# Attention with a gated feed-forward on one core: norm steps through PSUM, kept transposes, stored weight sums and another order of loads in the front stage

## The chip, the cores and the metric

One core of a Trainium2 chip runs the whole program in one launch. The metric is the device time of one execution in microseconds (us). Before the change three timed executions took 1230.99, 1231.0 and 1231.91 us, a median of 1231.0.

## The reference

The input `x` has 2048 rows of 512 in float32. With `xn` its layer norm (epsilon 1e-5, no scale or offset), the output is `x + s * g`:

```python
qkv = xn @ wqkv                      # 512 x 1536, 32 heads of 16
p = softmax(q @ k.T * 16 ** -0.5)    # every head, 2048 x 2048, no mask
s = (p @ v) @ wo                     # 512 x 512
h = relu(xn @ w1 + b1) ** 2          # 512 x 1792
g = silu(h @ w2 + b2)                # 1792 x 512
```

All inputs and the output are float32.

## The kernel before

Every large matrix product is made in three terms: an operand is cast to a "high" part in fp32r, what is left is its "low" part, and high x high, high x low and low x high are added up in PSUM. A split is thus a cast (mostly on ACT) and a subtraction (mostly on POOL).

The program has a **front stage** that normalizes x, transposes it and makes k, q and v, and then 64 **turns** of attention, into which the feed-forward network's matmuls are woven, and a short end. The order of every engine is written out by hand: an engine runs its instructions in the order in which the Python code issues them and waits by semaphore for what each needs. SP issues nearly all DMAs, also in order, and a DMA that waits holds those behind it.

The front stage works on four chunks of 512 rows:

- `norm` (L176) takes statistics on DVE (L181, L187), a square root on ACT (L191), then for each group of rows a few steps on numbers of 128x2 (L193 to L198: a reciprocal, one Newton step, the offset), all on DVE with operands in SBUF (`rs`, `mv`). From chunk 1 on ACT applies them as scale and offset (L204, tile `T`). It is a generator: the caller sets with `next` where the pieces stand among other work.
- `transpose` (L227) turns 256 rows by eight TensorE transposes into two PSUM tiles `D`, casts the high part on ACT (L238) and subtracts on DVE (L243). `transpose_tile` does so for the first two blocks of chunk 0, through a PSUM tile `B`. Even chunks lie in `KA0` (high) and `KA1` (low), odd ones in `xh`, `xl`.
- v is made per 128 rows by twelve matmuls (`start_value`, `end_value`, L117), evicted to one of three blocks `P10` to `P12` and stored (`vd`).
- k and q of a pair of chunks (0 and 1, then 2 and 3) are made by a scheme of seven products in place of eight (the Winograd form of Strassen's). It needs four sums of weight quarters for each of four kinds, k and q by two halves p (`sums_w`, L340 to L343, DVE; split by `split_sums`, L110), and four sums of transposed x (`sums_x`, L311 and L326 on DVE, cast L320, low part POOL L311). `first_products` and `second_products` work on the even chunk alone (L377, L388), `last_products` makes the rest for one kind: five groups of six matmuls (L291) with six DVE additions (L415) that free the PSUM banks, each result split (L104, L110) and stored (`kd`, `qd`).

PSUM tiles `B` and `D` have four banks each, taken in turn. `first_half(c)` holds what is done for the odd chunk c: products of the even chunk, splits of sums, transposes, x sums and values. After `first_half(1)` come the four `last` of the first pair, with chunk 2's norms, transposes and values between, then `first_half(3)` and the last four `last_products`.

The weight sums of the first pair of kinds (k, p = 0 and 1) are computed for chunks 0 and 1 and computed again for chunks 2 and 3 (`more_sums(0, 4)` and `sums_w(*kinds[1])`, read from `QA0` and `QA1`, which hold raw k weights). Those of q are split once, stored to DRAM (`sd`, L361) and loaded for the second pair (L366). Of the raw q weights (`wr`) rows 0 to 255 are split on ACT and POOL (L104, L172), rows 256 to 511 later on DVE (L106, L172, `engs=(dve, dve)`). In `sums_x` the whole transposed x of the even chunk is had as high + low, so that each sum with it takes two subtractions or additions.

The SP queue toward the end of the front stage carries, in order: stores of k, loads of the q sums of p = 1, two pieces of w1 (`wr`), v stores, the q sums of p = 0, q stores, the first k block of attention (`KA0`), k stores, the first q block (`QA0`), v and a second k block.

Of the kernel before, what the change touches and what calls it, by code (L numbers as in the profile page):

```python
# [34 lines left out]
EPS = 1e-5  # L35
# [12 lines left out]
@with_exitstack  # L48
def mha_ffn_kernel(ctx: ExitStack, tc: tile.TileContext, x, wqkv, wo, bx, w1, b1, w2, b2, out):
    nc = tc.nc  # L50
    x, out = x[0], out[0]
    ctx.enter_context(tc.manual_schedule())
    keep = ctx.enter_context(tc.tile_pool(name="keep", bufs=1))
    dram = ctx.enter_context(tc.tile_pool(name="dram", bufs=1, space=DRAM))

    ident = keep.tile([128, 128], FT, name="ident")
    make_identity(nc, ident)
    nvalid = keep.tile([1, 1], I32, name="nvalid")
    stat = keep.tile([128, 80], FT, name="stat")
# [5 lines left out]
    sdram = {p: dram.tile([128, 2, 4, 2, 128], FT, name=f"sd{p}") for p in range(2)}  # L65

    udram = [[dram.tile([2, 2, 16, 4, 512], FT, name=f"ud{g}_{c}") for c in range(NC)] for g in range(4)]
    zdram = [[dram.tile([4, 512], FT, name=f"zd{q}_{c}") for c in range(NC)] for q in range(NQ)]
    gdram = dram.tile([S, D], FT, name="gd")

    with tc.tile_pool(name="sb", bufs=1) as sb, ExitStack() as banks:
        fast_path(tc, sb, banks, locals())
    general_path(tc, dram, nvalid, ident, vdram, kdram, qdram, gdram, x, wo, out)


def fast_path(tc, sb, banks, env):
# [52 lines left out]
    b2b = t([128, D], FT, "b2b")  # L129

    xload, xnorm, wraw, wsp, xT = {}, {}, {}, {}, {}
    plain, both, wsp2 = {}, [], {}

    def load_x(c):
        for i in range(2):
# [38 lines left out]
    def norm(c, tiles):  # L174

        n = len(tiles)  # L176
        xin = [xload[c, j // 2][:, j % 2] for j in tiles]
        st = t([128, n, 6], FT, "st")
        mv = t([128, n, 2], FT, "mv")
        for j in range(n):  # L180
            dve.bn_stats(st[:, j], xin[j])  # L181
            if c == 0:
                yield
        if c:
            yield
        for j in range(n):
            dve.bn_aggr(mv[:, j], st[:, j])  # L187
        s = t([128, 4, n], FT, "rs")
        sd, r, e, b = (s[:, j] for j in range(4))
# [4 lines left out]
        dve.scalar_tensor_tensor(e, r, -0.5, r, op0=OP.mult, op1=OP.mult)  # L194
        dve.scalar_tensor_tensor(e, var, EPS, e, op0=OP.add, op1=OP.mult)
        dve.scalar_tensor_tensor(r, e, 1.5, r, op0=OP.add, op1=OP.mult)
        if c:
            dve.scalar_tensor_tensor(b, mv[:, :, 0], -1.0, r, op0=OP.mult, op1=OP.mult)  # L198
        for j in range(n):
            m = tiles[j]  # L200
            if m % 2 == 0:
                xnorm[c, m // 2] = t([128, 2, 512], FT, "T") if c < 2 else xload[c, m // 2]
            if c:
                act.activation(xnorm[c, m // 2][:, m % 2], xin[j], AF.Identity, bias=b[:, j:j + 1],  # L204
                               scale=r[:, j:j + 1])
# [21 lines left out]
    def transpose(c, i):  # L227
# [8 lines left out]
        s = slice(256 * i, 256 * i + 256)  # L236
        for j in range(2):
            act.copy(h[j][:, :, s], halves[j])  # L238
        if c % 2:
            plain[c, i] = halves, [t([128, 2, 2, 256], FT, f"P{2 + 2 * i + j}") for j in range(2)]  # L240
# [4 lines left out]
    def transpose_tile(i):  # L245

        pt = t([128, 4, 128], FT, "B")
        for k in range(4):
            nc.tensor.transpose(pt[:, k], xnorm[0, 0][:, i, 128 * k:128 * k + 128], ident)
        s = slice(128 * i, 128 * i + 128)  # L250
        act.copy(both[0][:, :, s], pt)
        dve.tensor_tensor(both[1][:, :, s], pt, both[0][:, :, s].bitcast(FT), op=OP.subtract)

    def xpart(c, p, k):
        return xT[c][p][k // 2][:, k % 2]
# [45 lines left out]
    def sums_x(c, i, between=lambda: None):  # L301

        s = slice(256 * i, 256 * i + 256)
        if i == 0:
            for m, tags in enumerate((("y0", "y1"), ("u0", "u1"), ("P14", "P15") if c == 1 else ("T", "T"),
                                       ("V0", "V1") if c == 1 else ("P11", "P12"))):
# [4 lines left out]
        sub = lambda o, a, b, eng=dve: eng.tensor_tensor(o, a, b, op=OP.subtract)  # L311
        sub(t1, f[0], h[0])
        sub(t1, t1, l[0])
        sub(t2, f[1], t1)
        sub(t3, f[1], t3)
        between()
# [5 lines left out]
                sub(tforms[m][1][:, :, s], v, tforms[m][0][:, :, s].bitcast(FT), pool)  # L322

        def fourth():
            sub(t4, h[1], t2)
            dve.tensor_tensor(t4, t4, l[1], op=OP.add)  # L326
            parts_of([(3, t4)])

        parts_of([(1, t2), (0, t1), (2, t3)])
        return fourth  # L330

    sraw, halves_of_k = {}, []

    def sums_w(which, p, tag="gl"):

# [9 lines left out]
    def sum_tiles(which, p, tags):  # L345

        if len(tags) == 1:
            ev = t([128, 2, 4, 2, 128], FR, tags[0])
            parts = ev[:, 0], ev[:, 1]
        else:  # L350
            parts = [t([128, 4, 2, 128], FR, tag) for tag in tags]
        sforms[which, p] = [[a[:, m] for a in parts] for m in range(4)]
        return parts

    def split_sums(which, p, tags):

        raw, parts = sraw.pop((which, p)), sum_tiles(which, p, tags)
        split(*parts, raw, act, pool)
        if which == "q":
            for a, part in enumerate(parts):  # L360
                sp.dma_start(sdram[p][:, a], part.bitcast(FT))  # L361

    def load_sums_w(p, tags):

        for a, part in enumerate(sum_tiles("q", p, tags)):
            sp.dma_start(part.bitcast(FT), sdram[p][:, a])  # L366

    def first_products(c, which, ps=range(2)):

# [287 lines left out]
    split_w("v", (0, 1))  # L657
    load_w("q", sp)
    xT_tiles(0)
    transpose_tile(0)  # L660
    keep_clock(3)
    next(parts[2])
    transpose_tile(1)
    split_w("v", (2, 3), "h")
    next(parts[2])
    run(parts[2])
# [15 lines left out]
    more(third, 4)  # L682
    for j in range(2):
        end_value(0, j, firsts[j])
    next(parts[0])
    next(parts[1])
    end_value(0, 2, third)
    save_xT(0)
    sp.dma_start(b2b, b2.partition_broadcast(128))

# [8 lines left out]
            next(parts, None)  # L699

    kinds = [(which, p) for which in "kq" for p in range(2)]
    sets = (("KA2",), ("P6", "P7")) * 3 + (("P8", "P9"), ("V1", "QA1"))
    next(parts[1])
    next(parts[0])
    sums_w(*kinds[0])
    values_of_chunk(0, (3,))
    split_w("q", (0, 1))
# [3 lines left out]
    next(parts[1])  # L711
    sums_w(*kinds[1], "V0")

    def more_sums(n, use):
        sums_w(*kinds[n])
        split_sums(*kinds[n], sets[use])

    def first_half(c):
        both_t1 = t([128, 2, 512], FT, "P13")
# [3 lines left out]
            f()  # L723
        if c == 1:
            split_sums(*kinds[0], sets[0])
        split_sums(*kinds[1], sets[1])
        if c == 3:
            load_sums_w(1, sets[7])
            for _ in range(2):
                load_piece()  # L730
        if c == 1:
            split_w("q", (2, 3), engs=(dve, dve))
        for i in range(2):
            first_products(c - 1, "q", (i,))
            transpose(c, i)
# [13 lines left out]
        made[1]()  # L749

    def steps_of(parts, n=1):
        for _ in range(n):
# [34 lines left out]
    turn["KA"] = -1  # L787
    load_ka(0, 0)

    for n, (which, p) in enumerate(kinds):  # L790
        if n == 1:
            load_qa(0, 0)
            load_v(0)
            load_ka(0, 1)
        if n == 3:
# [28 lines left out]
    def finish(n):  # L824
# [17 lines left out]
        events.setdefault(2 * n + 2, []).insert(0, (load_sums, (qd, qc)))  # L842
        events.setdefault(2 * n + 3, []).insert(0, (rowsums, (qd, qc)))

    def check(z, n):
# [4 lines left out]

    sums = {}

    def load_sums(qd, qc):
# [453 lines left out]
```

## Time and profile before

The profiled execution took 1232.14 us; its span, from the first instruction to the last, is 1230.4 us.

| | |
|---|---|
| median of three timed executions | 1231.0 us |
| profiled execution / its span | 1232.14 / 1230.4 us |
| mean granted TensorE clock | 0.997 |
| busy share PE / ACT / DVE / POOL | 98% / 85% / 71% / 29% |
| front stage (to the first attention matmul) | 0 to 149.1 us |
| DMA, mean over the span | 122 GB/s |

PE is TensorE's matmuls, PEld its weight loads, DVE VectorE, ACT ScalarE, POOL GpSimd, SP the engine whose queue issues DMAs. A row of the timeline has the start in us, the time in us, the engine, the line (L) of the kernel, the operation, output<-inputs by tile names without their numbers, the shapes, a count (neighbouring instructions of one kind are merged), and in brackets the idle time before it and what ended that. A row of the waits has waiter <- releaser: us in total, times, longest. A row of a window has its length and then, per engine, busy us and the number of instructions, then the granted clock, the busy share of the DMA engines and GB/s. A row of the groups ends in busy us, mean ns of one, and idle time before them.

### The profile page before, as it was taken

Reading aid. Unit: us, or ns where it says so; the run is one execution under the profiler, and the core shown is the slowest. Engines: PE = TensorE matmul, PEld = TensorE weight load, DVE = VectorE, ACT = ScalarE, POOL = GpSimd, SP = SyncE. Lnnn points to the kernel's source line nnn. Section 1 sums busy time; section 2 is a strip of 40 time slices with the busy share of each in tenths; the row PEclk is TensorE's granted clock in tenths of the full one; section 3 lists DMA queues with packets and bytes.
Section 4 is the critical chain, followed back from the end, with each engine's and each line's share of the span. In section 5 each row is a group of like instructions: output and inputs, shape, how many; then the busy total and the mean of one; then the engine's idle time right before and its main releaser. Section 6 shows DMA issues by size and latency. Waiting matters only on the chain.

```text
span 1230.4 us, 24207 instructions
## 1 busy us (share of the span) xinstructions
PE 1209.7 (98%) x9877; PEld 712.9 (58%) x9877; DVE 874.4 (71%) x1369; ACT 1041.4 (85%) x1225; POOL 356.3 (29%) x268
## 2 busy tenths in 40 slices
PE   9898999999999999999999999999999999999996
PEld 8676755555555555555555555555555555555553
DVE  7968677666767775757676766676775758777776
ACT  5545398889999899888998988899899899899983
POOL 5746732122220230404022222131330403321222
PEclk9999999999999999999999999999999999999999
DMA  7577843322161323223523214151422233465444
GB/s 286 209 276 268 274 175 106 83 66 92 42 189 43 110 79 100 79 75 90 173 62 112 61 45 135 27 173 49 135 79 78 75 100 79 130 194 160 151 140 102
DMA packets 106424, 150.71 MB, mean 122 GB/s; under 512 B 43258, under 2 KB 57608, under 8 KB 106308
## 3 DMA queue, kind: packets, MB, share of 16 engines
q1 hardware_dynamic: 103652, 140.74, 36.3%
q0 software_dynamic: 2368, 7.87, 2.2%
q8 instruction: 78, 1.28, 0.5%
q10 hardware_dynamic: 288, 0.52, 0.1%
q14 instruction: 38, 0.31, 0.1%
HBM read 101.51 MB, written 47.57 MB: 121 GB/s over the span
## 4 chain that ended last, share of the span: by engine, by line
PE 87%; DVE 1%; issue 1%; DMA 0%; POOL 0%; SPq 0%; ACT 0%; DVEq 0%; POOLq 0%
PE acc L811 36%; PE S L519 28%; PE S L471 14%; PE acc L471 4%; PE lin L471 2%; PE B L291 1%; DMA hl<-gd 0%; PE S L954 0%; PE B L117 0%; PE lin L291 0%; SPq L841 0%; PE acc L291 0%; POOL P L311 0%; POOL T L311 0%; POOL u L311 0%
## 5 line engine op out<-in xcount | busy, mean ns | idle before, releaser
L475 ACT ACTIVATE P<-S 128x1024 f32<-128x1024 f32 x702 | 663.0, 1035 | 94.7 <-PE S L471 92.8
L811 PE MATMUL acc<-P,V 128*32 128x512 f32 x4096 | 453.5, 594 | 0.0
L494 DVE COPY P<-acc 128x512 f32<-128x512 f32 x322 | 222.7, 692 | 141.0 <-PE lin L471 68.5
L475 ACT ACTIVATE P<-P 128x1024 f32<-128x1024 f32 x322 | 314.5, 1082 | 0.0
L811 PEld LDWEIGHTS acc<-P,V 128*32 128x32 f32 x4096 | 126.1, 110 | 287.5 <-issue 265.5
L471 PE MATMUL S<-QA,KA 64*128 64x512 f32 x1404 | 291.9, 404 | 0.0
L494 DVE COPY P<-lin 128x512 f32<-128x512 f32 x322 | 220.5, 685 | 2.3 <-PE lin L471 0.6
L471 PEld LDWEIGHTS S<-QA,KA 64*128 64x128 f32 x1404 | 134.5, 184 | 108.4 <-issue 41.8
L471 PE MATMUL acc<-QA,KA 64*128 64x512 f32 x322 | 127.3, 395 | 0.2 <-DVE seen L1063 0.2
L471 PE MATMUL lin<-QA,KA 64*128 64x512 f32 x322 | 127.4, 396 | 0.0
L110 POOL TENSOR_TENSOR wf1l<-wr,wf1h 128x1024 fp32r<-128x1024 f32 x28 | 68.5, 2446 | 176.7 <-DVE wf1h L106 108.2
L545 POOL MEMSET note<- 1x1 f32 x68 | 6.0, 88 | 385.8 <-PE S L519 369.4
L519 PE MATMUL S<-xl,wf1h 64*128 64x512 f32 x464 | 96.5, 391 | 0.0
L110 POOL TENSOR_TENSOR hl<-T,hh 128x1024 fp32r<-128x1024 f32 x28 | 80.1, 2862 | 52.9 <-DVE hh L106 52.9
L110 POOL TENSOR_TENSOR wf2l<-wr,wf2h 128x1024 fp32r<-128x1024 f32 x28 | 67.2, 2400 | 90.4 <-DVE wf2h L106 90.4
L519 PE MATMUL S<-xh,wf1l 64*128 64x512 f32 x480 | 92.0, 391 | 0.0
L519 PE MATMUL S<-wf2l,hh 64*128 64x512 f32 x448 | 90.9, 390 | 0.0
L837 DVE TENSOR_TENSOR ou<-acc,ou 128x512 f32<-128x512 f32 x31 | 21.4, 692 | 97.1 <-PE acc L811 93.2
L519 PE MATMUL S<-wf2h,hl 64*128 64x512 f32 x448 | 83.8, 391 | 0.0
L519 PE MATMUL S<-xh,wf1h 64*128 64x512 f32 x480 | 78.0, 392 | 0.0
L519 PE MATMUL S<-wf2h,hh 64*128 64x512 f32 x448 | 72.1, 394 | 0.0
L471 PEld LDWEIGHTS acc<-QA,KA 64*128 64x128 f32 x322 | 59.4, 184 | 16.3 <-DVE P L494 2.3
(353 smaller groups left out, 1467.1 us busy)
## 6 DMA issues: line engine op xcount, KB each, us to landing
wr<-in_B_w_dram SPq DMA_DIRECT2D x56, 512.0 KB
KA<-kd SPq DMA_DIRECT2D x64, 256.0 KB
QA<-qd SPq DMA_DIRECT2D x128, 128.0 KB
u<-ud SPq DMA_DIRECT2D x15, 512.0 KB
kd<-P SPq DMA_DIRECT2D x11, 512.0 KB
V<-vd SPq DMA_DIRECT2D x8, 664.0 KB
qd<-P SPq DMA_DIRECT2D x9, 512.0 KB
vd<-P SPq DMA_DIRECT2D x16, 280.0 KB
```

The lines of the kernel that those rows point to most:

```text
L110: leng.tensor_tensor(lo, src, hi.bitcast(FT), op=OP.subtract)
L291: mm(dst, left[a][:, k], right[b][:, k], start=n == 0, stop=n == 5)
L471: mm(dst, k[r, p, 128 * (kb % 8):128 * (kb % 8) + 128], q[r, p], start=True, stop=True)
L475: act.activation(ptile[i, p], src, AF.Exp, scale=SCALE)
L494: dve.tensor_copy(ptile[i, p][:, hp], sides[hp])
L519: ins = mm(bank, self.lhs(a, k)[r], self.rhs(b, k)[r], start=n == 0 and self.at[other] == 0, stop=n == len(self.todo[half]) - 1 and self.a ...
L545: f = pool.memset(note[:, notes[0]:notes[0] + 1], 0.0)
L811: mm(sides[0][32 * j:32 * j + 32], vq[qd][:, kb, 17 * j:17 * j + 32], ptile[i, j // 2][:, j % 2], start=first, stop=last)
L837: dve.tensor_tensor(ou, sides[0], part[0], op=OP.add)
```

## The change

Four edits, all in the front stage; no attention turn is touched.

1. **Norm steps.** For chunks 1 to 3 two temporaries of `norm` lie in a PSUM tile `D`, and seven DVE steps stand where five were. Each step with two tensor operands has one of them in PSUM.
2. **Chunk 0's transposes kept whole.** `transpose_tile` and `transpose` copy chunk 0's transposed x unsplit to `V1` and `P4` (`raw0`; six more ACT copies), and `sums_x(1)` takes its sums from there: one DVE operation in place of two, four times.
3. **All weight sums kept in DRAM.** The sums of all four kinds are stored (`save_sums`; those of k at the end of `first_half(1)`) and loaded for chunks 2 and 3 (`load_sums`), in place of being computed again for k. `QA0` and `QA1` are free earlier and take x sums of chunks 1 and 3.
4. **Other order.** The whole q weights are split on ACT and POOL, before the norms of chunk 1 are through. In `first_half(3)` SP loads both k sums and the first q block first, then the first k block after the x sums, then both q sums and only then the two pieces of w1.

```diff
 def norm(c, tiles):
...
+        if c:
+            small = t([128, 512], FT, "D")
+            first, e2 = small[:, :n], small[:, n:2 * n]
...
         dve.reciprocal(r, sd)
-        dve.scalar_tensor_tensor(e, r, -0.5, r, op0=OP.mult, op1=OP.mult)
-        dve.scalar_tensor_tensor(e, var, EPS, e, op0=OP.add, op1=OP.mult)
-        dve.scalar_tensor_tensor(r, e, 1.5, r, op0=OP.add, op1=OP.mult)
         if c:
-            dve.scalar_tensor_tensor(b, mv[:, :, 0], -1.0, r, op0=OP.mult, op1=OP.mult)
+            dve.reciprocal(first, sd)
+            dve.scalar_tensor_tensor(e, var, EPS, first, op0=OP.add, op1=OP.mult)
+            dve.scalar_tensor_tensor(e2, e, -0.5, first, op0=OP.mult, op1=OP.mult)
+            dve.scalar_tensor_tensor(b, mv[:, :, 0], -1.0, first, op0=OP.mult, op1=OP.mult)
+            dve.scalar_tensor_tensor(r, e2, 1.5, r, op0=OP.add, op1=OP.mult)
+            dve.scalar_tensor_tensor(b, e2, 1.5, b, op0=OP.add, op1=OP.mult)
...
 def sums_x(c, i, between=lambda: None):
...
-        sub(t1, f[0], h[0])
-        sub(t1, t1, l[0])
+        if c == 1:
+            sub(t1, f[0], raw0[0][:, :, s])
+        else:
+            sub(t1, f[0], h[0])
+            sub(t1, t1, l[0])
...
     split_w("k")
+    for dst, src in copies:
+        act.copy(dst, src)
...
     for j in range(2):
         end_value(0, j, firsts[j])
+    split_w("q", (0, 1))
     next(parts[0])
     next(parts[1])
     end_value(0, 2, third)
+    split_w("q", (2, 3))
...
 def first_half(c):
...
         if c == 1:
             split_sums(*kinds[0], sets[0])
-        split_sums(*kinds[1], sets[1])
-        if c == 3:
-            load_sums_w(1, sets[7])
-            for _ in range(2):
-                load_piece()
-        if c == 1:
-            split_w("q", (2, 3), engs=(dve, dve))
+            split_sums(*kinds[1], sets[1])
+        else:
+            load_sums(0)
+            load_sums(1)
+            load_qa(0, 0)
...
+        if c == 3:
+            turn["KA"] = -1
+            load_ka(0, 0)
         values_of_chunk(c, (3,))
         if c == 3:
-            load_sums_w(0, sets[6])
+            load_sums(2)
+            load_sums(3)
+            for _ in range(2):
+                load_piece()
         made[1]()
+        if c == 1:
+            for n in range(2):
+                save_sums(n)
...
     last(1, 2)
-    more_sums(0, 4)
     last(1, 3)
     steps_of(parts, 3)
-    sums_w(*kinds[1])
     first_half(3)
```

How this moves instructions is seen best at three places. First DVE, in the last two `last` of the first pair, where chunk 3's second norm stands; `xl` and `ou` are the additions that free PE's banks, `gl` the sums computed again, `rs`, `mv` and `D` the norm's numbers. Before:

```order
L181 BN_STATS st_161_993<-T_140_841 128x6 x2
L340 TENSOR_TENSOR gl_1001<-QA_9_174,QA_10_175 128x256
L341 TENSOR_TENSOR gl_1001<-gl_1001,QA_9_174 128x256
L342 TENSOR_TENSOR gl_1001<-QA_9_174 128x256
L343 TENSOR_TENSOR gl_1001<-QA_10_175,gl_1001 128x256
L415 TENSOR_TENSOR xl_166_1009<-B_168_1017,ou_85_517 128x512
L187 BN_AGGR mv_162_994<-st_161_993 128x2 x2
L415 TENSOR_TENSOR xl_166_1009<-B_170_1029,xl_166_1009 128x512
L193 RECIPROCAL rs_169_1027<-rs_169_1027 128x2
L194 SCALAR_TENSOR_TENSOR rs_169_1027<-rs_169_1027 128x2
L195 SCALAR_TENSOR_TENSOR rs_169_1027<-mv_162_994,rs_169_1027 128x2
```

The same place with the change (its line numbers are those of the changed kernel):

```order
L180 BN_STATS st_168_1018<-T_146_863 128x6 x2
L438 TENSOR_TENSOR xl_170_1025<-B_172_1033,ou_89_533 128x512
L192 BN_AGGR mv_175_1043<-st_168_1018 128x2 x2
L438 TENSOR_TENSOR xl_170_1025<-B_176_1047,xl_170_1025 128x512
L196 RECIPROCAL rs_173_1041<-rs_173_1041 128x2
L198 RECIPROCAL D_174_1042<-rs_173_1041 128x2
L199 SCALAR_TENSOR_TENSOR rs_173_1041<-mv_175_1043,D_174_1042 128x2
L200 SCALAR_TENSOR_TENSOR D_174_1042<-rs_173_1041,D_174_1042 128x2
L201 SCALAR_TENSOR_TENSOR rs_173_1041<-mv_175_1043,D_174_1042 128x2
L202 SCALAR_TENSOR_TENSOR rs_173_1041<-D_174_1042,rs_173_1041 128x2
L203 SCALAR_TENSOR_TENSOR rs_173_1041<-D_174_1042,rs_173_1041 128x2
```

The four sums ahead of the first addition are gone (four more behind this piece too), and the steps now read or write `D`.

Second DVE at the start of `first_half(1)`: `u` are chunk 0's second products of k, `hh` and `hl` the high and low q weights, `xl` the low part of chunk 1. Before:

```order
L388 TENSOR_TENSOR u_69_459<-B_68_452,P_65_435 128x512
L388 TENSOR_TENSOR u_71_468<-B_70_461,P_65_435 128x512
L106 CAST hh_59_412<-wr_32_249 128x512
L172 TENSOR_TENSOR hl_61_414<-wr_32_249,hh_59_412 128x512
L106 CAST hh_59_412<-wr_32_249 128x512
L172 TENSOR_TENSOR hl_61_414<-wr_32_249,hh_59_412 128x512
L243 TENSOR_TENSOR xl_79_498<-D_81_500,xh_77_496 128x2x256
L243 TENSOR_TENSOR xl_80_499<-D_82_501,xh_78_497 128x2x256
```

With the change:

```order
L411 TENSOR_TENSOR u_73_479<-B_72_472,P_69_455 128x512
L411 TENSOR_TENSOR u_75_488<-B_74_481,P_69_455 128x512
L256 TENSOR_TENSOR xl_83_514<-D_85_516,xh_81_512 128x2x256
L256 TENSOR_TENSOR xl_84_515<-D_86_517,xh_82_513 128x2x256
L256 TENSOR_TENSOR xl_83_514<-D_91_542,xh_81_512 128x2x256
```

The four splits have left DVE; the casts now stand on ACT and the subtractions on POOL, ahead of the work on `u` there.

Third SP in `first_half(3)`: `sd`, `sdk` and `sdq` are the stored sums, `KA2`, `P6` to `P9`, `P11`, `P12`, `V1` and `QA1` their places, `QA0` and `KA0` attention's first blocks. Before:

```order
L366 DMA V1_186_1124<-sd1_98 128x1024
L366 DMA QA1_187_1125<-sd1_98 128x1024
L572 DMA wr0_188_1128<-in_B_w1_dram 128x4x256
L572 DMA wr1_189_1130<-in_B_w1_dram 128x4x256
...
L278 DMA vd_93<-P10_13_185 128x560
L366 DMA P8_222_1304<-sd0_97 128x1024
L366 DMA P9_223_1305<-sd0_97 128x1024
L282 DMA qd0_2_79<-P0_215_1207 128x1024
L282 DMA qd2_2_87<-V0_217_1216 128x1024
L448 DMA KA0_225_1314<-kd0_0_69 32x2x1024 x4
```

With the change:

```order
L389 DMA KA2_189_1135<-sdk0_97 128x1024 x2
L389 DMA P6_190_1138<-sdk1_98 128x1024
L389 DMA P7_191_1139<-sdk1_98 128x1024
L478 DMA QA0_192_1142<-qd0_0_77 32x2x512 x4
...
L471 DMA KA0_224_1304<-kd0_0_69 32x2x1024 x4
L292 DMA vd_93<-P10_13_187 128x560
L389 DMA P8_226_1324<-sdq0_99 128x1024
L389 DMA P9_227_1325<-sdq0_99 128x1024
L389 DMA P11_228_1328<-sdq1_100 128x1024
L389 DMA P12_229_1329<-sdq1_100 128x1024
L595 DMA wr0_230_1332<-in_B_w1_dram 128x4x256
```

The rows left out are v stores; a second piece of w1 follows. `KA0` has moved ahead of the last v store and the q sums, the pieces of w1 (`wr`) behind them, and `QA0` from behind `KA0` to the head.

More of the change, by code (lines that the diff above doesn't have):

```diff
@@ L64, in mha_ffn_kernel @@
     xdram = [dram.tile([128, 2, 4, 512], FT, name=f"xd{c}") for c in range(3)]
-    sdram = {p: dram.tile([128, 2, 4, 2, 128], FT, name=f"sd{p}") for p in range(2)}
+    sdram = {(a, p): dram.tile([128, 2, 4, 2, 128], FT, name=f"sd{a}{p}") for a in "kq" for p in range(2)}
     udram = [[dram.tile([2, 2, 16, 4, 512], FT, name=f"ud{g}_{c}") for c in range(NC)] for g in range(4)]
@@ L131, in fast_path @@
     xload, xnorm, wraw, wsp, xT = {}, {}, {}, {}, {}
-    plain, both, wsp2 = {}, [], {}
+    plain, both, wsp2, raw0 = {}, [], {}, []
     def load_x(c):
@@ L238, in transpose @@
             act.copy(h[j][:, :, s], halves[j])
+        if c == 0:
+            for j in range(2):
+                act.copy(raw0[j][:, :, s], halves[j])
         if c % 2:
-            plain[c, i] = halves, [t([128, 2, 2, 256], FT, f"P{2 + 2 * i + j}") for j in range(2)]
+            plain[c, i] = halves, [t([128, 2, 2, 256], FT, f"QA{j}" if c == 1 and i else f"P{2 + 2 * i + j}")
+                                    for j in range(2)]
             act.copy(plain[c, i][1][1][:, 0], halves[0])
@@ L252, in transpose_tile @@
         dve.tensor_tensor(both[1][:, :, s], pt, both[0][:, :, s].bitcast(FT), op=OP.subtract)
+        return [(raw0[j][:, :, s], pt[:, 2 * j:2 * j + 2]) for j in range(2)]
     def xpart(c, p, k):
@@ L305, in sums_x @@
             for m, tags in enumerate((("y0", "y1"), ("u0", "u1"), ("P14", "P15") if c == 1 else ("T", "T"),
-                                       ("V0", "V1") if c == 1 else ("P11", "P12"))):
+                                       ("V0", "V1") if c == 1 else ("QA1", "V1"))):
                 tforms[m] = [t([128, 2, 512], FR, tag) for tag in tags]
@@ L324, in fourth @@
         def fourth():
-            sub(t4, h[1], t2)
-            dve.tensor_tensor(t4, t4, l[1], op=OP.add)
+            if c == 1:
+                sub(t4, raw0[1][:, :, s], t2)
+            else:
+                sub(t4, h[1], t2)
+                dve.tensor_tensor(t4, t4, l[1], op=OP.add)
             parts_of([(3, t4)])
@@ L352, in sum_tiles @@
         sforms[which, p] = [[a[:, m] for a in parts] for m in range(4)]
+        sumtiles[which, p] = parts
         return parts
@@ L358, in split_sums, with save_sums, load_sums @@
         split(*parts, raw, act, pool)
[L359 to L366, printed above, removed]
+    def save_sums(n):
+        for a in range(2):
+            sp.dma_start(sdram[kinds[n]][:, a], sumtiles[kinds[n]][a].bitcast(FT))
+    def load_sums(n):
+        for a, part in enumerate(sum_tiles(*kinds[n], sets[4 + n])):
+            sp.dma_start(part.bitcast(FT), sdram[kinds[n]][:, a])
     def first_products(c, which, ps=range(2)):
@@ L659, in fast_path @@
     xT_tiles(0)
-    transpose_tile(0)
+    raw0 += [t([128, 2, 512], FT, tag) for tag in ("V1", "P4")]
+    copies = transpose_tile(0)
     keep_clock(3)
     next(parts[2])
-    transpose_tile(1)
+    copies += transpose_tile(1)
     split_w("v", (2, 3), "h")
@@ L701, in fast_path @@
     kinds = [(which, p) for which in "kq" for p in range(2)]
-    sets = (("KA2",), ("P6", "P7")) * 3 + (("P8", "P9"), ("V1", "QA1"))
+    sets = (("KA2",), ("P6", "P7")) * 3 + (("P8", "P9"), ("P11", "P12"))
     next(parts[1])
     next(parts[0])
+    next(parts[1])
+    values_of_chunk(0, (3,))
     sums_w(*kinds[0])
-    values_of_chunk(0, (3,))
-    split_w("q", (0, 1))
     bp = t([128, 14], FT, "D")
```

22 lines of the change are left out of this document (12 added, 10 removed).

## The prediction

> **What bounds the kernel now.** I read the page first: the busy shares and the chain that ended last.
>
> ```profile
> PE 1209.7 (98%) x9877; PEld 712.9 (58%) x9877; DVE 874.4 (71%) x1369; ACT 1041.4 (85%) x1225; POOL 356.3 (29%) x268
> PE 87%; DVE 1%; issue 1%; DMA 0%; POOL 0%; SPq 0%; ACT 0%; DVEq 0%; POOLq 0%
> ```
>
> PE sets the end, so a front-stage edit is worth only the PE idle time that it removes (the order on PE is the same in both programs, bar tile names). Stretches of 10 us show where PE is short of matmuls:
>
> ```profile
> 30.00:40.00 10.00, 8.23 (x39) 6.32 (x38) 9.90 (x11) 5.68 (x11) 7.58 (x4) 1.00 0.74 241
> 90.00:100.00 10.00, 6.96 (x29) 5.01 (x28) 9.69 (x17) 4.03 (x8) 5.12 (x3) 1.00 0.89 356
> 130.00:140.00 10.00, 10.00 (x44) 8.08 (x43) 5.25 (x8) 3.17 (x6) 8.57 (x8) 1.00 0.96 332
> 170.00:180.00 10.00, 10.00 (x90) 7.30 (x90) 7.71 (x14) 10.00 (x11) 0.22 (x3) 1.00 0.07 26
> ```
>
> The second number is PE busy, then its matmul count. 130 to 140 is full: 44 in 10 us, 0.227 us each. 30 to 40 and 90 to 100 are not; later in the run, as at 170, PE is full, and a gain in the front should reach the end whole. The list of PE's waits up to 165 us names each hole:
>
> ```profile
> PE B L291 <- DVE xl L415: 4.1, 2, 2.7
> PE D L234 <- ACT T L204: 1.7, 1, 1.7
> PE B L291 <- DVE hl L172: 1.6, 1, 1.6
> ...
> PE D L291 <- POOL P L110: 0.8, 1, 0.8
> PE B L117 <- ACT y L320: 0.6, 1, 0.6
> PE B L291 <- POOL P L311: 0.3, 1, 0.3
> PE B L291 <- DVE hh L106: 0.2, 1, 0.2
> ```
>
> That is 9.3 us in eight waits (left out: PE's very first wait, on the identity).
>
> **The change part by part.**
>
> *Norm steps with a PSUM operand.* The 1.7 us wait, on the timeline:
>
> ```profile
> 51.04 2.53 POOL L311 TENSOR_TENSOR V<-P,V 128x512 fp32r<-128x512 f32 x2
> 51.08 0.69 DVE L415 TENSOR_TENSOR xh<-B,P 128x512 f32<-128x512 f32 x1 [1.01 <-PE B L291]
> 52.38 1.21 DVE L195 SCALAR_TENSOR_TENSOR rs<-mv,rs 128x2 f32<-128x2 f32 x1
> 54.61 0.62 PE L291 MATMUL B<-V,wf2l 128*128 128x512 f32 x2
> 56.10 1.52 ACT L204 ACTIVATE T<-T,rs 128x512 f32<-128x512 f32 x2 [5.70 <-DVE rs L198]
> 56.97 1.36 PE L234 MATMUL D<-ident,T 128*128 128x128 f32 x8 [1.74 <-ACT T L204]
> 62.24 0.16 DVE L196 SCALAR_TENSOR_TENSOR rs<-rs 128x2 f32<-128x2 f32 x1
> ```
>
> A 128x2 step takes 0.16 us (62.24), but 1.21 at 52.38, ending at 53.59 with POOL's pair (51.04 + 2.53 = 53.57). The 128x512 add at 51.08, with one input in PSUM, runs its 0.69 under the same POOL work. So a DVE step with both tensors in SBUF waits for POOL, and one with a PSUM operand doesn't. Afterwards seven steps stand in place of five; all five two-tensor ones have a PSUM operand. PSUM cost of a 128x2 step isn't shown: at least 0.16, at most the 0.69 of a 128x512 add; I take 0.17, seven make 1.2 us. DVE takes them up at about 51.7 and ends near 53; the two activations of the ACT row (1.52) make T by 54.5, before PE is through with the matmuls from 54.61. The wait goes. Next late would be PE's own products.
>
> The gap measures more than the list says: from 54.61 to 56.97 is 2.36 us for two matmuls worth 0.45, so 1.9; the list counts from the drawn end and is 0.17 short per wait. It also costs clock:
>
> ```profile
> 58.00:60.00 2.00, 2.00 (x10) 1.56 (x8) 1.90 (x6) 0.62 (x1) 0.77 (x1) 0.64 0.11 43
> 60.00:62.00 2.00, 2.00 (x6) 1.61 (x5) 1.93 (x4) 0.81 (x2) 1.60 (x2) 0.51 0.13 51
> 98.00:100.00 2.00, 0.39 (x2) 0.00 (x0) 1.79 (x6) 0.95 (x2) 0.41 (x1) 1.00 0.40 156
> ```
>
> Granted clock 0.64 and 0.51 (third number from the end) over 4 us: 2 x 0.36 + 2 x 0.49 = 1.7 us lost right behind the gap. Term: 1.9 + 1.7 = **3.6**. [...]
>
> *Weight sums kept in DRAM.* Between 90 and 106 DVE makes the first pair's sums again:
>
> ```profile
> L194 DVE SCALAR_TENSOR_TENSOR rs<-rs 128x2 f32<-128x2 f32 x2 | 3.5, 1736 | 0.1
> L342 DVE TENSOR_TENSOR gl<-QA 128x256 f32<-128x256 f32 x2 | 3.0, 1516 | 0.0
> L341 DVE TENSOR_TENSOR gl<-gl,QA 128x256 f32<-128x256 f32 x2 | 3.0, 1490 | 0.1
> ```
>
> Four of the eight sums take 3.0 + 3.0 us, two steps of the norms another 3.5, all in front of the adds (L415) that free PE's banks. Without them DVE has, per 30 matmuls of PE (6.8 us), six adds (6 x 0.69 = 4.1), statistics of two tiles (some 1.5, as two such passes) and seven steps (1.2): it just keeps up, by my count with the last add about a microsecond ahead of its bank's next use. Both L415 waits go: 4.1 + 2 x 0.17 = **4.4**. In chunk 3 ACT also loses a 1024-wide cast ahead of the halves, and DVE is earlier by its sums; so the value tile's bank behind the 0.6 us wait (freed by DVE, behind those halves) comes over a microsecond sooner: **0.8**.
>
> The price is on SP and the DMA engines: four tiles of 128x1024 f32, 2.1 MB, stored near 54 us (four issues on SP, ahead of the kd stores) and read back near 108. The read-back has over 10 us before its first product. The second pair's reload keeps its place:
>
> ```profile
> 128.57 0.88 SPq L366 DMA_DIRECT2D P<-sd  x2
> 137.48 0.62 PE L291 MATMUL B<-xh,P 128*128 128x512 f32 x2
> ```
>
> 8.9 us from issue to use; but 1 MB of sums, 1 MB of w1 pieces and, ahead of them, KA now share this stretch. I take it as in time; the bound is rival 3. QA's four issues leave SP's crowded 138 to 143, which helps nobody who waits.
>
> *q weights split on ACT and POOL.*
>
> ```profile
> 32.56 2.75 DVE L172 TENSOR_TENSOR hl<-wr,hh 128x512 fp32r<-128x512 f32 x1
> 16.15 5.06 POOL L172 TENSOR_TENSOR wf2l<-QA,wf2h 128x512 fp32r<-128x512 f32 x4
> 24.49 2.76 POOL L172 TENSOR_TENSOR hl<-wr,hh 128x512 fp32r<-128x512 f32 x2 [3.28 <-ACT hh L104]
> 26.02 1.51 DVE L342 TENSOR_TENSOR V<-QA 128x256 f32<-128x256 f32 x1
> 27.46 0.41 DVE L343 TENSOR_TENSOR V<-QA,V 128x256 f32<-128x256 f32 x1
> ```
>
> DVE loses its four splits; the waits on hl and hh go (1.6 + 0.2 + 2 x 0.17 = 2.1). But POOL now goes from wf2l (16.15 + 5.06 = 21.2) straight into four hl (twice 2.76), to about 26.7, and beside it a 128x256 sum takes 1.51 instead of 0.41. The eight first sums, begun after the norm steps near 23, get four through by 27 and end near 29 instead of 27.9; the two L388 behind them, and ACT's casts behind those, slip by 1.1 to 1.5, and the third value tile's bank comes about 0.4 late. Term: **1.7**.
>
> *Raw transposes of chunk 0.* Six more ACT copies:
>
> ```profile
> 15.01 1.08 ACT L238 CAST KA<-D 128x512 fp32r<-128x512 f32 x2 [1.36 <-PE D L234]
> 17.35 0.59 ACT L104 COPY P<-B 128x512 f32<-128x512 f32 x1 [1.26 <-PE B L117]
> ```
>
> Four 128x256 copies at 0.3 to 0.4 fill the 1.36 us idle before 15.01, two of 0.54 the 1.26 before 17.35. I charge **-0.2** (bounds 0 and -0.6, if they run one behind the other at 0.5). They spare DVE four SBUF-only operations between 38 and 48, which hides behind values on PE and only keeps POOL's chain level with it.
>
> *The rest.* The 0.8 us wait hangs on this:
>
> ```profile
> 75.61 0.96 SPq L278 DMA_DIRECT2D vd<-P  x2
> 83.58 0.59 ACT L104 COPY P<-B 128x512 f32<-128x512 f32 x1 [6.99 <-DMA vd<-P]
> 84.22 0.76 PEld L291 LDWEIGHTS B<-V,hh 128*128 128x128 f32 x4 [0.41 <-ACT P L104]
> ```
>
> ACT waited 7 us for a v store to free its block, and the sum split behind it came late; the bank that it frees is PE's at 84.22. DVE's faster steps bring the kd stores, queued on SP ahead of it, about 2 us sooner against PE: 0.8 of 1.0 goes. Of the 0.5 on POOL's L311 at 129 I take 0.2: its chain starts from a value tile's eviction, and that moves with PE.
>
> Sum: 3.6 + 4.4 + 0.8 + 1.7 - 0.2 + 0.8 + 0.2 = 11.3. The profiled execution took 1232.14 (span 1230.4, 1.7 outside), 1.1 above the median of 1231.0; 1232.14 - 11.3 = 1220.8, and I say **1221.0**, for the margins under half a microsecond.
>
> **Rivals.** 1: POOL's unbroken split holds DVE longer (each of eight sums at 1.5): another 2 us late, PE waits for banks at the values and then for POOL's V at 51.04, which in this trace ends at 53.57, 0.1 before PE's group that reads it (54.61 less four matmuls). It costs 2 + 1: 1223.8. For it: the 1.51 row. Against: only the sums that start before 26.5 are hit.
>
> 2: the half clock isn't owed to that gap, or falls behind another: 1.7 less, 1222.5. For it: the 98 to 100 row, an emptier stretch at full clock; against: the fall right behind this gap and nowhere else in the rows. [...]
>
> 3: the reload at 128.57 lands late. The v store above took 8.0 us from issue to release under load, which would still do; 2 MB more beside it at 356 GB/s (the 90 to 100 row's last number) add 5.6 if all share: 128.57 + 8.0 + 5.6 = 142.2, a wait of 4.7, 1225.5. Against: those are issued behind it.
>
> 4: the PSUM operand frees nothing. Seven steps of up to 1.2: the gap grows by 2.4, the second L415 wait keeps 2.4, the 0.8 stays; 1.7 - 2.4 + 2.0 + 0.8 - 0.2 + 0.2 = 2.1 is left, 1230.0. Against: the row at 51.08.
>
> 5, the other side: the 2.1 MB of stores hold up the v store that ACT waits for at 83.58. The window rows:
>
> ```profile
> 52.00:54.00 2.00, 2.00 (x10) 1.59 (x10) 1.93 (x3) 0.00 (x0) 2.00 (x3) 1.00 0.00 0
> 78.00:80.00 2.00, 2.00 (x10) 1.61 (x9) 1.52 (x4) 0.00 (x0) 0.29 (x1) 1.00 0.84 195
> ```
>
> At 195 GB/s, 2.1 MB are 10.8 us, all of them passed on if none hides: the copy starts at 94.4, PE's fourth product of that pass (84.22) lacks its bank for 10.8 us, and half clock follows (1.7): 12.5 against 10.5 of other gains, 1234.1. It decides from a delay of some 9 us. Against: DMA shares of 0.00, 0.11 and 0.13 between 52 and 62 leave room for most of it.
>
> **How the numbers follow.** Forecast (1218.5 to 1223) 0.60, rival 1 0.12, rival 2 0.10, rival 3 0.06, rival 4 0.04, rival 5 0.08. The range 1217.5 to 1226.5 holds the forecast and the first three, 0.88, with the unknown costs. Rivals 1 to 3 and the forecast are faster by over 0.2% (2.5 us, about what a measurement can tell from no change): 0.88; rival 4 is within, 0.04; rival 5 slower, 0.08.
>
> **What would show it.** Right: steps of about 0.17 us on DVE under POOL; no PE wait on T, hl or the L415 adds; a granted clock of 1.00 through 50 to 70; the attention matmuls some 11 us sooner. Wrong: a PE wait at the values of chunk 1 (rival 1), a clock under 1.00 (2), at the third pass of chunk 3 (3), on T again (4), or ACT idle on a v store for over 9 us (5).

## The result and the profile after

The changed kernel took 1218.28 us (median of four executions, 1218.18 to 1218.44) against 1231.1 us for the kernel before (four, 1230.99 to 1231.91) on the same chip: a ratio of 0.9895, 95% interval 0.9877 to 0.9912. The forecast was 1221.0. The profiled execution took 1218.33 us with a span of 1216.6.

The page's busy line, the same windows as before, and the whole list of PE's waits up to 165 us:

```profile
PE 1205.6 (99%) x9877; PEld 714.0 (59%) x9877; DVE 846.7 (70%) x1365; ACT 1042.8 (86%) x1231; POOL 350.4 (29%) x268
```

```profile
30.00:40.00 10.00, 10.00 (x49) 8.10 (x47) 4.81 (x8) 7.28 (x14) 7.39 (x5) 1.00 0.73 226
90.00:100.00 10.00, 10.00 (x53) 8.42 (x52) 4.06 (x7) 6.11 (x12) 4.58 (x4) 1.00 1.02 376
...
58.00:60.00 2.00, 2.00 (x10) 1.62 (x9) 1.26 (x3) 1.19 (x3) 1.29 (x1) 1.00 1.02 404
60.00:62.00 2.00, 2.00 (x14) 1.75 (x13) 1.86 (x4) 0.00 (x0) 0.00 (x0) 1.00 1.01 385
```

```profile
PE B L672 <- POOL ident masks.py:199: 1.4, 1, 1.4
PE B L117 <- ACT y L337: 0.2, 1, 0.2
```

PE holds 49 and 53 matmuls where it held 39 and 29; the clock is 1.00 where it was 0.64 and 0.51. Of the eight waits (9.3 us) none is left; beside PE's very first wait stands a new one of 0.2 us, at 40.4.

The work on DVE, POOL and ACT around chunk 2's first norm:

```profile
49.70 1.30 POOL L325 TENSOR_TENSOR V<-QA,V 128x512 fp32r<-128x512 f32 x1
49.93 0.16 DVE L199 SCALAR_TENSOR_TENSOR rs<-mv,D 128x2 f32<-128x2 f32 x1
50.52 0.16 DVE L203 SCALAR_TENSOR_TENSOR rs<-D,rs 128x2 f32<-128x2 f32 x1
50.71 1.53 ACT L213 ACTIVATE T<-T,rs 128x512 f32<-128x512 f32 x2 [3.22 <-DVE rs L203]
53.07 1.03 PE L243 MATMUL D<-ident,T 128*128 128x128 f32 x8
```

The steps run at 0.16 us beside a busy POOL, `T` is ready at 50.71 + 1.53 = 52.24, and the transposes at 53.07 wait for nothing.

PE's first attention score (64-row matmul on `QA`, `KA`) started at 149.09 us before and starts at 136.58 now, 12.5 sooner. Since the first transpose stood at 7.89 and stands at 7.44, I use the stretch between these two as the **front length** of every kernel (one profiled execution each): 141.20 us before, 129.14 after, 12.06 less. It leaves out how late x arrives, which moved between 6.68 and 7.89 over these profiles. The other part of the 13.8 us by which the spans differ is that start (0.45) and about 1.3 us behind the front (0.9 spread over the turns, 0.4 at the last stores), in code that is the same; the medians differ by 12.8. What those small pieces are was not settled. With the starts of the same matmuls in both traces laid side by side, the 12.06 us come as 1.7 up to 43 us (times of the kernel before), 3.7 from there to 62, 1.0 to 88, 4.6 to 101, 0.7 at 117 and 0.4 at 129.

### The profile page after: what moved, and what is told of

It is laid out like the page before. It is cut to its first block, busy times and chain, and to the rows that moved or that the text cites. A ratio compares the mean times of both kernels' runs of the same rounds, so it can differ in the third digit from the quotient of the medians.

```text
span 1216.6 us, 24228 instructions
## 1 busy us (share of the span) xinstructions
PE 1205.6 (99%) x9877; PEld 714.0 (59%) x9877; DVE 846.7 (70%) x1365; ACT 1042.8 (86%) x1231; POOL 350.4 (29%) x268
## 3 DMA queue, kind: packets, MB, share of 16 engines
HBM read 103.61 MB, written 49.67 MB: 126 GB/s over the span
## 4 chain that ended last, share of the span: by engine, by line
PE 96%; DVE 1%; POOL 1%; DMA 1%; issue 0%; SPq 0%; ACT 0%; DVEq 0%; POOLq 0%
PE acc L841 36%; PE S L542 28%; PE S L494 14%; PE acc L494 5%; PE B L305 5%; PE B L117 3%; PE lin L494 2%; PE D L305 1%; PE B L672 1%; DMA hl<-gd 1%; PE D L243 0%; PE S L984 0%; PE lin L305 0%; PE acc L305 0%; SPq L871 0%
```

## The experiments

The question was which edit earns what, and whether the reasons hold. Each kernel was timed in five rounds beside the kernel before; "gain" is the difference of the two medians taken together. The ratios' intervals are 2 to 4 us wide, so differences near 1.5 us rest on the front length and the waits, not on the medians.

| kernel | us | ratio to before (95%) | gain | front length |
|---|---|---|---|---|
| changed kernel | 1218.28 | 0.9895 (0.9877 to 0.9912) | 12.8 | 129.14 |
| e1 its steps in SBUF | 1227.29 | 0.9967 (0.9955 to 0.9979) | 4.0 | 137.21 |
| e2 its q split as before | 1219.78 | 0.9909 (0.9894 to 0.9924) | 11.5 | 130.72 |
| e3 no kept transposes | 1220.04 | 0.991 (0.9894 to 0.9925) | 11.3 | 130.78 |
| e9 its sums ahead of steps | 1221.97 | 0.9923 (0.9909 to 0.9936) | 8.8 | 133.32 |
| e10 its loads as before | 1218.1 | 0.9897 (0.9882 to 0.9912) | 12.7 | 129.71 |
| e11 sums stored twice | 1224.1 | 0.9941 (0.9928 to 0.9955) | 6.7 | 133.85 |
| e12 late low half | 1217.84 | 0.9898 (0.9882 to 0.9915) | 12.6 | 128.61 |
| before + e4 stored sums and loads | 1224.89 | 0.995 (0.9936 to 0.9963) | 6.4 | 134.81 |
| before + e5 PSUM steps | 1223.3 | 0.9937 (0.9924 to 0.9951) | 7.6 | 133.17 |
| before + e6 early q split | 1233.39 | 1.002 (1.001 to 1.003) | -2.5 | 143.52 |
| before + e7 both of these | 1225.09 | 0.9952 (0.9939 to 0.9966) | 5.8 | 135.41 |
| before + e8 both, and order | 1223.36 | 0.9941 (0.9927 to 0.9955) | 7.4 | 133.79 |

### e1: the steps' temporaries in SBUF

```diff
-        s = t([128, 4, n], FT, "rs")
+        s = t([128, 6, n], FT, "rs")
...
-            first, e2 = small[:, :n], small[:, n:2 * n]
+            first, e2 = s[:, 4], s[:, 5]
```

> The changed kernel (1218.3 us) with the two temporaries of the norm in SBUF in place of PSUM; the same seven steps, in the same place, and the PSUM banks are taken in the same turn. Theory A (a DVE step with both tensors in SBUF waits for POOL, one with a PSUM operand does not): the five two-tensor steps take 1 to 1.2 us each again wherever POOL works, so T of chunk 1 comes 3 to 5 us later, PE waits 2 to 4 us on T near 53 and the granted clock falls below 0.7 for some 4 us behind it (1.7 more); with chunk 3's steps late too, 1222 to 1226. If the half clock is not owed to the gap, 1.7 less. Rival B (the place of the operands does not matter, the gain came from removed work and order): steps of 0.16 us, no wait on T, 1218.3 within 0.5.

Measured 1227.29 us, front 8.1 longer: theory A, and more than its 4 to 8. Chunk 1's norm on the timeline of e1, which the forecast had not looked at, and PE's window behind it:

```profile
20.28 5.09 POOL L172 TENSOR_TENSOR hl<-wr,hh 128x512 fp32r<-128x512 f32 x4
20.77 0.14 DVE L198 RECIPROCAL rs<-rs 128x2 f32<-128x2 f32 x1
20.95 0.63 DVE L199 SCALAR_TENSOR_TENSOR rs<-mv,rs 128x2 f32<-128x2 f32 x1
21.61 1.23 DVE L200 SCALAR_TENSOR_TENSOR rs<-rs 128x2 f32<-128x2 f32 x1
22.77 2.62 DVE L201 SCALAR_TENSOR_TENSOR rs<-mv,rs 128x2 f32<-128x2 f32 x1
25.67 2.93 ACT L213 ACTIVATE T<-P,rs 128x512 f32<-128x512 f32 x4 [4.47 <-DVE rs L203]
29.12 1.91 PE L305 MATMUL B<-KA,wf2h 128*128 128x512 f32 x4 [3.67 <-ACT P L104]
```

```profile
30.00:32.00 2.00, 2.00 (x6) 1.63 (x5) 0.28 (x2) 0.65 (x2) 1.00 (x1) 0.50 0.33 129
```

The steps with two SBUF tensors wait for POOL (0.63, 1.23 and 2.62 us, where the changed kernel has 0.16 and 0.17); the reciprocal, with one, doesn't (0.14). (One input alone isn't the rule, as the last section shows.) ACT then waits 4.47 us for the last step with the evictions of PE's banks queued behind, so PE waits 3.7 and the clock halves (0.50 from 30 to 32). The wait on `T` (1.4 us) is back too. Nothing is lost at the adds near 100 or behind the v store: PE gains as much there as in the changed kernel. In the changed kernel the PSUM operand is thus what makes an unbroken POOL run affordable.

### e2 and e3: the q split, and the kept transposes, undone

```diff
-    split_w("q", (0, 1))
...
-    split_w("q", (2, 3))
...
+    split_w("q", (0, 1))
...
+            split_w("q", (2, 3), engs=(dve, dve))
```

> The changed kernel with the split of the q weights put back where it was: rows 0 to 255 on ACT and POOL behind the third value tile, rows 256 to 511 by four DVE instructions ahead of chunk 1's transposes. Theory A (a split on DVE stands ahead of PE's first q products and holds them): the waits on hl and hh of 2.1 us near 32 to 36 return, the 0.35 us wait at the third value tile's bank goes: 1220.0 to 1220.5. Rival B (DVE is ahead by now, since it is spared other work there): 1218.0, faster by the 0.35.

1219.78 us, front 1.6 longer. PE's waits in e2 are theory A's, a little smaller:

```profile
PE B L305 <- DVE hl L172: 1.4, 1, 1.4
PE B L672 <- POOL ident masks.py:199: 1.4, 1, 1.4
PE B L305 <- POOL hl L172: 0.2, 1, 0.2
```

In e3 the six copies go, and `sums_x(1)` takes high and low parts again:

```diff
-        if c == 1:
-            sub(t1, f[0], raw0[0][:, :, s])
-        else:
-            sub(t1, f[0], h[0])
-            sub(t1, t1, l[0])
+        sub(t1, f[0], h[0])
+        sub(t1, t1, l[0])
...
-    for dst, src in copies:
-        act.copy(dst, src)
```

> The changed kernel without the unsplit copies of chunk 0: six ACT copies fewer, and each of the four sums of chunk 1 that used them takes two SBUF-only DVE operations again. Theory A (DVE operations that have only SBUF operands wait for POOL there, and the norm steps and adds stand behind them): DVE comes 2 to 4 us later to the norm steps of chunk 2, of which 0.8 us is spare ahead of the transposes near 53: 1219.5 to 1221.5. Rival B (they hide behind values on PE, as forecast): the copies cost nothing and spare nothing, 1218.1 to 1218.5.

1220.04 us, front 1.6 longer: theory A. The last of the sums on DVE in e3, the first norm step behind them, and two of PE's waits:

```profile
44.31 0.68 DVE L321 TENSOR_TENSOR P<-KA,P 128x512 f32<-128x512 f32 x1
45.03 1.67 DVE L336 TENSOR_TENSOR P<-P,KA 128x512 f32<-128x512 f32 x1
46.63 1.78 DVE L321 TENSOR_TENSOR QA<-KA,QA 128x512 f32<-128x512 f32 x1
48.45 1.67 DVE L336 TENSOR_TENSOR QA<-QA,KA 128x512 f32<-128x512 f32 x1
52.03 0.15 DVE L196 RECIPROCAL rs<-rs 128x2 f32<-128x2 f32 x1
```

```profile
PE B L117 <- ACT y L330: 0.7, 1, 0.7
PE B L301 <- POOL V L321: 0.3, 1, 0.3
```

Four SBUF-only operations stand where two did; under POOL they take up to 1.78 us in place of 0.68, and the steps start at 52.03 in place of 49.67. That eats the 0.8 us spare ahead of the transposes.

### e4 and e5: stored sums alone, PSUM steps alone

Both start from the kernel before. e4 has the edits 3 and 4 of the change without the early q split; e5 has the diff of `norm` and nothing else.

> The kernel before (1231.1 us) with the stored weight sums and the new order of loads alone; norm steps in SBUF, q split on DVE, no kept copies. Theory A (sums and SBUF-only steps share the two waits on DVE's adds between 90 and 106; of the second wait the steps keep 2.4 us): 1231.1 - 2.1 - 0.8 for the value bank of chunk 3 = 1228.2, and one wait on an L415-type add remains near 100. Rival B (the sums alone make both waits): 1231.1 - 4.4 - 0.8 = 1225.9, no wait there. Rival C (2.1 MB more of stores and loads cost time that the other edits hide): a longer wait of ACT on a v store near 77 to 84 and of PE behind it, 1228 or more with both adds' waits gone.

> The kernel before (1231.1 us) with the norm steps through PSUM alone; sums computed again, q split on DVE. Theory A (PSUM operands free the steps from POOL): steps of 0.15 to 0.2 us, no wait on T near 57, granted clock 1.00 from 56 to 62 (3.6 us), the second add's wait near 101 shorter by up to 2.4, the wait behind the v store shorter by 0.8: 1224.5 to 1227.5. If the half clock is not owed to the gap: 1.7 more. Rival B (operand place does not matter): two steps more in every norm, 1231 to 1233.

e4: 1224.89 us, front 6.4 shorter; both waits on the adds are gone (rival B), and so is that on POOL's L311. Theory A had the steps keep 2.4 us there, but only one of the four two-tensor steps was held:

```profile
91.60 0.17 DVE L194 SCALAR_TENSOR_TENSOR rs<-rs 128x2 f32<-128x2 f32 x1
91.80 1.21 DVE L195 SCALAR_TENSOR_TENSOR rs<-mv,rs 128x2 f32<-128x2 f32 x1
93.05 0.16 DVE L196 SCALAR_TENSOR_TENSOR rs<-rs 128x2 f32<-128x2 f32 x1
```

Rival C fell: ACT's wait for the v store was 6.55 us (7.0 before). e5: 1223.3 us, front 8.0 shorter, better than any case that was written down. No wait on `T`, no half clock (1.00 from 20 to 112), no wait behind the v store, and the adds' waits went from 4.1 to 1.3 us (the row is e5's):

```profile
PE B L300 <- DVE xl L424: 1.3, 2, 0.8
```

The sums and the steps stand in one DVE queue ahead of the same adds, so each edit alone takes away most of that wait. The two single gains (6.4 + 7.6 = 14.0) count it twice.

### e6 to e9: the early q split and the order of the steps

e6 moves the whole q split, as the change does, into the kernel before; e7 adds PSUM steps; e8 adds this move, which the change has too, though its diff ahead of the prediction leaves it out:

```diff
-    sums_w(*kinds[0])
+    next(parts[1])
     values_of_chunk(0, (3,))
+    sums_w(*kinds[0])
...
-    next(parts[1])
```

> The kernel before (1231.1 us) with the whole q weights split on ACT and POOL early, nothing else. Theory A: the waits on hl and hh (2.1 us) go, up to 0.4 comes back at a value bank: 1229.0 to 1229.5. Rival B (POOL's unbroken split holds DVE, whose norm steps and sums with SBUF operands then come 2 us and more late): the wait on T near 57 grows by as much, 1230.5 to 1233.

> The kernel before (1231.1 us) with both: norm steps through PSUM, and the q weights split early on ACT and POOL. If the parts add up: the sum of the two single differences, to 0.5 us. If the q split alone costs what it saves because SBUF-only steps behind POOL come late, the pair gains over 1 us more than the sum of the two.

> The kernel of the run before (norm steps through PSUM and the early q split, 1225.1 us) with one thing more: chunk 1's second group of norm steps stands ahead of the weight sums on DVE, as in the changed kernel. Theory A (the early split holds the sums behind POOL, the steps queued behind those sums are late, and ACT and PE with them; the order takes the steps out of that queue): the 2.5 us wait near 29 and the half clock behind it (about 1.5) go, 1221 to 1222. Rival B (ACT's evictions are late for another reason, that the kept transposes cure): the wait stays, 1225.

e6 is slower than before by 2.5 us (1.002, 1.001 to 1.003): rival B's sign, just above its range, though the price falls in chunk 1's norm near 30 and not at `T`, where the wait is 1.5 in place of 1.7. e7 gains 5.8. Its two parts add up to 5.1 by the medians (7.6 - 2.5) and to 5.7 by the front lengths (8.0 - 2.3), so the two simply add up as far as these figures can tell: PSUM steps by themselves don't make the early split pay, and e7 gains 1.8 less than PSUM steps alone. DVE, ACT and PE in e7:

```profile
20.67 5.58 POOL L172 TENSOR_TENSOR hl<-wr,hh 128x512 fp32r<-128x512 f32 x4
21.16 1.07 DVE L349 TENSOR_TENSOR gl<-QA,QA 128x256 f32<-128x256 f32 x1
22.27 1.40 DVE L350 TENSOR_TENSOR gl<-gl,QA 128x256 f32<-128x256 f32 x1
23.59 1.50 DVE L351 TENSOR_TENSOR gl<-QA 128x256 f32<-128x256 f32 x1
25.02 1.51 DVE L352 TENSOR_TENSOR gl<-QA,gl 128x256 f32<-128x256 f32 x1
26.54 0.15 DVE L196 RECIPROCAL rs<-rs 128x2 f32<-128x2 f32 x1
27.62 1.52 ACT L213 ACTIVATE T<-P,rs 128x512 f32<-128x512 f32 x2 [4.41 <-issue]
29.05 1.04 ACT L386 COPY P<-B 128x512 f32<-128x512 f32 x2
29.66 1.64 PE L300 MATMUL B<-KA,hh 128*128 128x512 f32 x4 [2.50 <-ACT P L386]
```

The steps are fast now (0.14 to 0.17 us), but four sums held by POOL (1.07 to 1.51 us) stand ahead of them; ACT waits 4.41 us for the last step, with PE's bank behind. (The row names "issue"; the activation starts as DVE's steps, from 26.54 on, end.) With the steps ahead of the sums (e8) that wait is gone and 1.6 us come back (5.8 to 7.4), short of the 3 to 4 expected: what is left are e3's waits (0.7 on `y`, 0.3 on POOL's `V`) and those on the sums made again. So even with PSUM steps and the better order the early split earns nothing over PSUM steps alone (gain 7.4 against 7.6, front 133.79 against 133.17). That it earns 1.6 in the changed kernel (e2) fits e3's waits: without the kept transposes PE loses at chunk 1's sums what it gained at the split. The early split with kept transposes but computed sums was not run.

> The changed kernel with the first four weight sums put back ahead of the last value tile of chunk 0 and of the second group of norm steps. Theory A (order is a part of the gain, as above): a PE wait of about 2.5 us near 29 and 1.5 us of half clock, 1222 to 1222.5. Rival B (order costs nothing where the steps go through PSUM): 1218.3.

The same move, undone in the changed kernel: 1221.97 us, front 4.2 longer, as theory A had it, with a PE wait of 3.1 us near 30. Its five executions spread from 1219.63 to 1223.52, with mean granted clocks of 0.998 for the two shortest and 0.995 to 0.996 for the others.

### e10 and e11: the loads, and twice the stores

e10 puts the w1 pieces, `KA0` and `QA0` near their old places; e11 adds this line in `save_sums`:

```diff
+            sp.dma_start(env["s2dram"][kinds[n]][:, a], sumtiles[kinds[n]][a].bitcast(FT))
```

> The changed kernel with the loads of chunk 3 near their old order: the pieces of w1 behind the k sums, the first k block behind the first half, the first q block behind k stores. Theory A (the order of loads buys nothing, PE waits for none of them): 1218.0 to 1218.8 and no PE wait on a load. Rival B (the order of loads is a part of the 2 us by which stored sums gave more than its two waits): 1219.3 to 1221, with a PE wait on KA or QA near 137.

> The changed kernel with each of the eight stores of weight sums issued twice, the second to other DRAM: 4.2 MB more, of which 2.1 MB near 54 to 62. Theory A (DMA and SP have room there): 1218.0 to 1218.8; ACT's wait for a v store near 77 grows, PE's wait near 81 by under 0.5 us. Rival B (the fifth rival of the prediction: stores hold up the v store that ACT waits for, decided from some 9 us of delay): ACT's wait grows from 5.9 to over 9 us and PE waits 1 to 6 us near 81: 1219.5 to 1225.

e10: 1218.1 us and no wait on a load: the order of loads buys nothing here. Its front is 0.57 longer than 129.14 after the earliest start but one (6.70), in pieces of 0.1 to 0.3. e11: 1224.1 us, front 4.7 longer. ACT's and PE's rows in e11, and PE's window behind them:

```profile
81.29 0.58 ACT L105 COPY P<-B 128x512 f32<-128x512 f32 x1 [10.21 <-DMA vd<-P]
```

```profile
81.93 1.61 PE L306 MATMUL B<-V,hh 128*128 128x512 f32 x3 [3.19 <-ACT P L105]
```

```profile
82.00:84.00 2.00, 2.00 (x5) 1.61 (x6) 1.66 (x9) 1.52 (x3) 1.10 (x1) 0.50 1.03 422
```

This is the fifth rival's mechanism in full, in answer to 2.1 MB more near 54 to 62: the wait for the v store goes from 5.92 to 10.21 us, PE waits 3.2, and half clock follows. In the changed kernel the same copy reads:

```profile
76.77 0.59 ACT L104 COPY P<-B 128x512 f32<-128x512 f32 x1 [5.92 <-DMA vd<-P]
```

So the stores are hidden there with about a microsecond to spare (4.3 later at ACT made 3.2 at PE), not with the nine that the rival's text may suggest, which was the delay at which the sign would turn.

### e12: the low half later

```diff
-    split_w("q", (2, 3))
+    split_w("q", (2, 3), "h")
...
+    pool.tensor_copy(t([128, 1], FT, "okm"), sraw[kinds[1]][:, 3, 0, :1])
+    split_w("q", (2, 3), "l")
```

> The changed kernel with POOL's last two q splits (rows 256 to 511) put behind the eight first weight sums on DVE, by a one-column copy on POOL that reads the last sum; POOL is idle there from 25.8 to 30.1 us. Theory A (DVE's first sum waits through POOL's whole unbroken run, and that delay is what makes the third value tile's bank late at 40.4): the sum waits to 23.3 and no longer to 26.1, the eight sums end near 26.5 in place of 28.8, the 0.35 us at 40.4 goes: 1217.9, which the times can't tell from 1218.3, but the trace can. Rival B (the delayed splits push POOL's work on u, and with it all of POOL behind it, back by up to 1 us): 1218.5 to 1219.5, PE waiting for POOL's V near 52 or for T near 53.

Theory A. The changed kernel's row for the first sum, then e12's:

```profile
23.12 2.98 DVE L360 TENSOR_TENSOR gl<-QA,QA 128x256 f32<-128x256 f32 x1
```

```profile
22.54 0.48 DVE L360 TENSOR_TENSOR gl<-QA,QA 128x256 f32<-128x256 f32 x1
25.96 2.56 POOL L172 TENSOR_TENSOR hl<-wr,hh 128x512 fp32r<-128x512 f32 x2
```

The eight sums end at 25.7 in place of 28.8, 2.3 sooner beyond the earlier start, the new wait at 40.4 is gone, and the front is 0.5 shorter. At 1217.84 us it is the fastest kernel here, but the times (1217.02 to 1218.35) can't tell it from the changed one.

## Why the prediction was right, point by point

The net came out as foreseen: a sum of 11.3 us against 12.06 in the front, by removing PE's holes one by one, and no hole of size took their place. But the sum was made by holes, and the prices of single edits that it implies were in part wrong.

- **PE bounds, and a front gain reaches the end whole**: right, 12.5 us at the first score and 13.4 at the last DVE instruction.
- **Norm steps, 3.6**: as a hole, right (a gap of 1.9 and the clock behind it; 3.7 in starts of matmuls). Alone the edit takes 8.0 off the front (e5), since the same steps also stand ahead of the v store's bank and of the adds: 3.9 at this hole, 1.2 at that bank, 2.9 at the adds near 100. Undone it costs 8.1 of front (e1), but at other places: 5.3 at chunk 1's evictions near 29 with the half clock behind them, 2.2 at `T` and 0.7 at 69, less the 0.5 of the wait at 40.4, and nothing at the adds, which the stored sums had freed. The price of 0.17 per step was right (0.15 to 0.17 beside a busy POOL); that the term covered one norm of six was not said.
- **Stored sums, 4.4 and 0.8**: right (4.6 and 0.7 in starts). The 0.2 for POOL's L311 at 129 was 0.4: that wait too goes with the sums (e4), and stays with PSUM steps (e5).
- **q split, 1.7**: as a hole right (2.1 in starts, less 0.5 at 40.4; forecast 2.1 and 0.4). The step that failed is the cover: the prediction let only the eight sums be late by POOL's run and looked for the price at `V` and the value bank. Alone the edit costs 2.5 us (e6), through the norm steps and ACT's evictions behind them. What makes it pay in the changed kernel is three things together: PSUM steps (e1), a moved `next(parts[1])` (e9) that the prediction gave no term, and, as e8 beside e3 suggests, the kept transposes.
- **Raw transposes, -0.2**: the wrong sign. The copies cost nothing, and without them PE loses 1.6 us (e3). "Hides behind values on PE" failed: the SBUF-only operations delay the steps (52.03 in place of 49.67) and POOL's `V` (PE waits 0.3 for it).
- **v store, 0.8**: right in size (PE's loss near 81 fell from 1.1 to 0.3), and its cause holds: with PSUM steps alone it goes, with stored sums alone 0.8 stays.
- **Rivals**: 1 and 5 are real mechanisms that stood just outside this kernel (e6, e11); 4 is refuted (e1); 2 is not needed, since the clock stayed at 1.00, and e4, which keeps the gap at `T` (a wait of 1.8), keeps the half clock behind it (0.86, 0.50 and 0.79 over 56 to 62), while e5 has neither; 3 found no wait: the reload issued at 112.62 was used at 124.93 without one.

## What to carry to other kernels

A hole on the bounding engine gives the worth of the whole change, but not of an edit: before a busy engine is given a longer unbroken run, list every instruction of the engine that it holds off, and what is queued behind each on a third engine. Two edits that shorten one queue share its wait, so gains taken singly don't add up, and an edit that costs alone can earn in company. Where a transfer hides, measure its margin by doubling it.

## What the runs showed of the hardware

DVE operations on two SBUF tensors waited for POOL, and those with a PSUM operand didn't: the three steps that took 0.63, 1.23 and 2.62 us in e1 took 0.16 and 0.17 in the changed kernel, and of its 128x512 sums beside POOL the one with `D` took 0.68 (at 103.66) and the next, on SBUF alone, 1.51 (at 104.38). One SBUF input is no safe side: the reciprocal (0.14 us in e1) didn't wait, but a 128x512 cast did, 1.50 us in place of 0.41 (kernel before):

```profile
28.99 0.41 DVE L106 CAST hh<-wr 128x512 fp32r<-128x512 f32 x1
29.20 3.04 POOL L397 TENSOR_TENSOR u<-u 128x512 fp32r<-128x512 f32 x2 [1.95 <-ACT u L393]
31.02 1.50 DVE L106 CAST hh<-wr 128x512 fp32r<-128x512 f32 x1
```

What no row of the forecast had shown: against back-to-back POOL work a single DVE operation can wait through several instructions (2.98 us in the changed kernel, 2.62 in e1, 3.93 in e9, against 1.27 for one of POOL's), while in e7 the two took turns and DVE got one operation in for each of POOL's (four of 1.07 to 1.51 us beside POOL's four in 5.58). What decides between the two was not found.

Half clock (0.50 to 0.55 over the lowest 2 us) followed PE gaps (start to start, less the matmuls' own time) of 1.9 (before and e4), 2.1 (e6), 2.7 (e7), 3.2 (e9), 3.4 (e11) and 3.8 us (e1), but not those of 2.8 (before, at 101, and e6, at 103; 1.00 in both from 98 to 112), so no length of gap separates them. What decides was not found. The spread of e9's executions, 3.9 us with lower mean clocks in the longer ones, is more than the half clock in its trace, which is worth 1.7 us (granted clock 0.77, 0.50 and 0.87 over 30 to 36). Which execution loses the clock can't be seen without its trace. In the kernel before, lower mean clocks didn't come with longer times (1230.18 to 1232.09 us at 0.997, 1230.74 to 1232.64 at 0.995), so the 1.7 us of the norm steps' term is read from profiles alone.
